# A hand-numbered order, opening only: W, DAD and U products of the first superstep moved ahead of weight pieces and of the second superstep's first key product, a scan and a key load moved later

## The chip, the cores and the metric

One core of one Trainium2 chip runs the kernel. The metric is device time in microseconds (us), median of the runs; lower is better. All times below are us unless marked ns. Engines are called as in the profile: PE is TensorE (matmuls), PEld its weight loads, DVE is VectorE, ACT is ScalarE, POOL is GpSimd, SP is SyncE, which issues every DMA of this kernel.

## The reference

Two parts in a row: a linear-attention recurrence over 768 steps for 4 batches of 8 heads of 40 dimensions, and a feed-forward block on its output.

```
for t in range(S):
    y[:, :, t] = einsum('bhd,bhde->bhe', rt, state)
    Sa = einsum('bhde,bhe->bhd', state, at)
    state_decay = state * wt[:, :, None, :] - einsum('bhd,bhe->bhde', Sa, bt)
    state = state_decay + einsum('bhd,bhe->bhde', vt, kt)
...
x = attn_out.transpose(0, 2, 1, 3).reshape(3072, 320)
h = x @ w_in                      # 320 -> 2048
sp = maximum(h, 0) + log1p(exp(-abs(h)))
return (h * erf(sp)) @ w_out      # 2048 -> 320
```

## The kernel before, in words

**Tiling.** The recurrence is done in chunks of 32 steps. The 32 (batch, head) pairs are two groups of 16; a group's 768 steps are 6 supersteps of 128 steps, so there are 12 supersteps (numbered 0 to 11) of 4 chunks each. The feed-forward block follows one superstep behind: each superstep gives 256 tokens, which go through 16 column tiles of w_in (the products into `ph`, L823), a long ACT and DVE chain, and 16 row tiles of w_out (the products into `po`, L878).

**One superstep.** `prep` loads the decays `w` and makes two scans on DVE (suffix, L439, into `Wt`; prefix, L443 with a copy L444, back into `Pr`). `aphase`, once a chunk, loads the keys (`kba`, tile `bk`), multiplies the a part by the prefix (`ab`, L472) and the k and b part by the suffix (`bk`, L477: "turned keys"), forms the product `A` (L482, into `pA`), masks it (`Am`, L489), sends it to DRAM (`AD`) and transposes the keys (`bT`, L500, also into `pA`, copied out to `sg`). `tphase`, once a superstep, fetches all four chunks' masked products from DRAM (`Ti`), inverts 16x16 triangles by 28 short DVE operations (`Tm` and `Ts`, L529 and L530), sends the result to DRAM (`TD`) and back in another shape (`tb`), turns it by a DVE transpose (`R`, L538), and finishes 32x32 blocks by two groups of PE products with a copy between: `W` (L547, T x Ap into `pA`), `Wm` (the copy into tile `W`, L377), `DAD` (L547 again, Tb x W into `pA`), and `Tb` (a DVE add, L554). `chain`, once a chunk and strictly one after the other, carries the state: `Z` (L593), copy `zt`, `U` (L602: zt x Tb, needs `Tb` of the tphase), copy `us`, `UT` (L627), copy `vtu`, `PQ` (L636), mask `PQm` (L639), `MY` (L647 and L651), and the state add `MT` (L654).

**The opening.** Before the feed-forward block can begin, superstep 0 must go through all of this, and superstep 1's `aphase` and `tphase` run interleaved with superstep 0's four chains. In the same time the weights of the feed-forward block come in as 64 bit numbers and are made into two f32r parts: three integer DVE operations a piece (`w1`, `w3`, `w5`: L737 to L739), a rounding copy on ACT (`whi`, L743, or `whr`, L775), and for each half of a piece the product pair `wd_` on PE (L754 and L755: identity x value, minus identity x rounded value, into `ph` or `po`), copied out by `wlo`. 190 small `warm` products (L422) without a reader are strewn between.

**What sets the order.** Nothing at run time: `Plan.add` only numbers the operations, and `ORDER`, a table of all 4630 numbers, gives the order in which they are issued. Each engine runs its own operations strictly in that order; `ENGINES` says which engine each one runs on.

```
def emission(order):
    with tc.manual_schedule():
        for i in order:
            o = N.P.ops[i]
            o["fn"](o["eng"])
...
for c in range(NC):
    P.add("W", "PE", lambda e, c=c: mm(e, s.AP, W, c, lo), ["T"] + [("ap", j) for j in range(2)], ["pA"], pr, 0.32)
P.add("Wm", [("ACT", 0.37), ("DVE", 0.42)], lambda e: s.copy(e, s.W2[:, :, lo], pw[:, :, lo]), ["pA"], [("w2", 0)], pr)
for c in range(NC):
    P.add("DAD", "PE", lambda e, c=c: mm(e, s.W2, tb, c, up), [("w2", 0)] + ktb, ["pA"], pr, 0.32)
P.add("Tb", "DVE", ...
```

The last number of an `add` is a duration for a planner that is no longer in the file; it has no effect. `A`, `bT`, `W` and `DAD` of all supersteps share the PSUM tile `pA`, so each of them waits until the one before has been copied out.

Of the kernel before, what the change touches and what calls it, by code (L numbers as in the profile page):

```python
# [1008 lines left out]
```

## Time and profile before

| what | value |
|---|---|
| device time, three runs | 767.58, 760.24, 767.63; median 767.58 |
| profiled execution, first to last instruction (span) | 754.8 |
| profiled execution's own time | not given; the page has its span alone |
| PE busy over the span | 722.7 (96%) |
| DVE, ACT busy | 643.1 (85%), 573.3 (76%) |
| DMA | 94.63 MB, mean 125 GB/s |

The page's busy times are of one profiled execution. A busy PE is not a PE at its peak, and among its busy time are the `warm` products, which nobody reads. The span begins with the opening described above, in which PE is mostly filled with such products and everything waits for a chain of small steps; from the first product of the feed-forward block on (L823) PE works without longer pauses until the end.

### The profile page before, as it was taken

To read this page: it belongs to the slowest core of one execution; us is meant where nothing else is said; L and a number is where in the kernel's file an instruction comes from. 1 tells how busy PE (TensorE), PEld (TensorE's weight loads), DVE (VectorE), ACT (ScalarE), POOL (GpSimd) and SP (SyncE) were. 2 spreads that over 40 slices of the span, in tenths; PEclk is the share of its full clock that TensorE was granted. 3 is DMA by queue.
4 is the path that set the end of the run, shared out by engine and by line. 5 is a ranking of instruction groups with operands and counts; after the bars stand their busy time and mean duration, and the time that the engine had idled before them with its cause. 6 is when DMAs were issued, how large, how long until landed. Compare 5 with 4: busy or idle time off the path is not lost.

```text
span 754.8 us, 32087 instructions
## 1 busy us (share of the span) xinstructions
PE 722.7 (96%) x13807; PEld 570.4 (76%) x13807; DVE 643.1 (85%) x1461; ACT 573.3 (76%) x1122; POOL 5.6 (1%) x15
## 2 busy tenths in 40 slices
PE   9968899789999999999999999999999999999996
PEld 3645558668778778878878888887888787888874
DVE  8887878889879899998889899998997898878774
ACT  3322544987988998888898897898988888776992
POOL 2000000000000000000000000000000000000000
PEclk9988999999999999999999999999999999999999
DMA  8687566655564655555545556546545444312000
GB/s 255 175 256 197 142 160 153 144 124 122 129 147 121 131 140 126 118 125 126 131 126 136 132 134 139 130 104 138 140 103 115 124 112 92 104 41 61 21 17 22
DMA packets 165616, 94.63 MB, mean 125 GB/s; under 512 B 115452, under 2 KB 148988, under 8 KB 165468
## 3 DMA queue, kind: packets, MB, share of 16 engines
q1 hardware_dynamic: 165468, 92.51, 50.1%
q8 instruction: 110, 1.80, 1.1%
q14 instruction: 38, 0.31, 0.1%
HBM read 73.48 MB, written 14.16 MB: 116 GB/s over the span
## 4 chain that ended last, share of the span: by engine, by line
PE 83%; ACT 5%; DVE 5%; DMA 3%; issue 2%; SPq 1%; DVEq 0%
PE po L878 29%; PE ph L823 22%; PE my L647 4%; PE ph L422 4%; PE pA L547 4%; PE pQ L636 4%; PE pA L482 3%; PE my L602 2%; PE my L593 2%; PE pA L500 2%; PE pQ L618 2%; PE my L651 2%; SPq L381 1%; PE pQ L627 1%; ACT l L831 1%
## 5 line engine op out<-in xcount | busy, mean ns | idle before, releaser
L878 PE MATMUL po<-wo,h 128*128 128x320 f32 x768 | 265.2, 454 | 1.1 <-DVE h L869 1.1
L878 PEld LDWEIGHTS po<-wo,h 128*128 128x128 f32 x768 | 125.5, 189 | 30.5 <-DVE h L869 1.9
L831 ACT ACTIVATE l<-l 128x512 f32<-128x512 f32 x192 | 111.0, 624 | 8.3 <-DVE nd L856 7.5
L823 PE MATMUL ph<-xh,wih 128*128 128x256 f32 x384 | 113.8, 378 | 0.0
L823 PEld LDWEIGHTS ph<-xh,wih 128*128 128x128 f32 x384 | 69.5, 190 | 24.1 <-issue 0.3
L823 PE MATMUL ph<-xh,wil 128*128 128x256 f32 x384 | 77.2, 282 | 0.7 <-issue 0.7
L823 PE MATMUL ph<-xl,wih 128*128 128x256 f32 x384 | 76.9, 282 | 0.0
L856 DVE TENSOR_TENSOR nd<-l,r 128x512 f32<-128x512 f32 x96 | 64.3, 687 | 9.6 <-ACT r L831 8.4
L868 DVE TENSOR_TENSOR l<-l,r 128x512 f32<-128x512 f32 x96 | 64.5, 682 | 1.2 <-ACT l L831 0.4
L869 DVE SCALAR_TENSOR_TENSOR h<-l,h 128x512 f32<-128x512 f32 x96 | 64.6, 684 | 0.5
L857 DVE SCALAR_TENSOR_TENSOR r<-nd,r 128x512 f32<-128x512 f32 x96 | 64.2, 683 | 0.2
L831 ACT ACTIVATE l<-h 128x512 f32<-128x512 f32 x96 | 57.6, 627 | 4.2 <-DVE h L377 3.1
L823 PEld LDWEIGHTS ph<-xh,wil 128*128 128x128 f32 x384 | 59.5, 190 | 0.7 <-issue 0.7
L375 ACT COPY h<-ph 128x512 f32<-128x512 f32 x84 | 48.9, 583 | 14.2 <-PE ph L823 13.4
L823 PEld LDWEIGHTS ph<-xl,wih 128*128 128x128 f32 x384 | 59.2, 189 | 0.0
L831 ACT ACTIVATE r<-r 128x512 f32<-128x512 f32 x96 | 55.3, 623 | 0.4
L831 ACT ACTIVATE r<-l 128x512 f32<-128x512 f32 x96 | 54.9, 621 | 0.3
L422 PE MATMUL ph<-d 104*128 104x512 bf16 x190 | 53.3, 401 | 1.6 <-DVE d L392 1.6
L823 PE MATMUL ph<-xl,wir 128*128 128x256 f32 x192 | 54.2, 282 | 0.0
L823 PE MATMUL ph<-xh,wir 128*128 128x256 f32 x192 | 54.1, 282 | 0.0
L375 ACT COPY Zm<-MT 40x320 f32<-40x320 f32 x62 | 28.3, 457 | 28.7 <-DVE MT L654 24.1
L489 DVE TENSOR_TENSOR Zs<-pA,tri 64x256 f32<-64x256 f32 x96 | 40.6, 423 | 11.1 <-PE pA L482 6.0
(142 smaller groups left out, 1346.4 us busy)
## 6 DMA issues: line engine op xcount, KB each, us to landing
bk<-in_kba_e SPq DMA_DIRECT2D x46, 416.0 KB
vt<-in_rv_e SPq DMA_DIRECT2D x96, 120.0 KB
wo<-in_moe_w_in SPq DMA_DIRECT2D x10, 512.0 KB
h<-in_moe_w_out SPq DMA_DIRECT2D x10, 512.0 KB
Pr<-in_w_e SPq DMA_DIRECT2D x12, 419.7 KB
Rt<-in_r_e SPq DMA_DIRECT2D x48, 104.0 KB
Vu<-in_v_x SPq DMA_DIRECT2D x96, 40.0 KB
Zm<-in_v_s SPq DMA_DIRECT2D x48, 80.0 KB
```

The costliest lines, as they stand in the source:

```text
L375: self.nc.scalar.copy(o, i)
L422: P.add("warm", "PE", lambda e: nc.tensor.matmul(s.ph[1], s.d1[:, :128], s.d1[:, :512], start=True, stop=True), ["d1"], ["phw"], -1e3, 0.22)
L489: P.add("Am", "DVE", lambda e, x=x, xs=xs: nc.vector.tensor_tensor(out=zx[64:128, x], in0=pz[xs], in1=s.tri[xs, None, :].to_broadcast([64, ...
L547: nc.tensor.matmul(pw[js, i, ts], l[js, i], r[js, i, ts], start=True, stop=True)
L636: nc.tensor.matmul(pq[i % 2 * 64:i % 2 * 64 + 64, i // 4, i // 2 % 2], vr[:, 256 + n_ * 64:320 + n_ * 64], vr.rearrange("p (a x) -> p a x" ...
L823: nc.tensor.matmul(ph[:, j * 256:j * 256 + 256], a[:k, fs], b[:k], start=(m == 0), stop=(m == 7))
L831: self.P.add(name, "ACT", lambda e: nc.scalar.activation(out=o, in_=i, **kw), rd, wr + ["act"], pr, 0.62)
L856: P.add("nd", [("DVE", 0.69)], lambda e, r=r, l=l, nd=nd: s.eng(e).tensor_tensor(out=nd, in0=l, in1=r, op=ALU.mult), [("l", il), ("r", ir) ...
L857: P.add("rho", "DVE", lambda e, r=r, nd=nd: nc.vector.scalar_tensor_tensor(out=r, in0=nd, scalar=2 * C4, in1=r, op0=ALU.add, op1=ALU.mult) ...
L868: P.add("E", [("DVE", 0.69)], lambda e: s.eng(e).tensor_tensor(out=l, in0=l, in1=r, op=ALU.mult), [("r", ir)], [("l", il)], pr)
L869: P.add("G", "DVE", lambda e: nc.vector.scalar_tensor_tensor(out=h, in0=l, scalar=-1.0, in1=h, op0=ALU.add, op1=ALU.mult), [("l", il)], [( ...
L878: nc.tensor.matmul(po, h[:, bs], s.wo[:, f], start=(f == 0), stop=(f == 15))
```

## The change

Only the table `ORDER` changes (and both tables are wrapped at another width, which moves every line number below by 30: L547 of before is L577 after, and so on). 16 numbers of the 4630 stand in another place, all between the 254th and the 386th, that is within the opening. By operation:

- The prefix scan of superstep 1 (463) and its copy come after the 28 short operations of superstep 0's triangle inversion, not before them.
- The load of the second chunk's keys of superstep 1 (476, 416 KB) is issued after the `tb` loads of superstep 0, not before its `TD` stores.
- The four `W` products (310 to 313) stand together, `Wm` (314) follows them on DVE before two weight operations, and the four `DAD` (315 to 318) come next. The two `wd_` pairs of the weight piece with nd (399, 402), which stood before `W` and between `W` and `DAD`, come after `DAD`.
- `U` of chunk 0 (522) with its copy `zt` (521) comes before superstep 1's first `A` (469); it stood after `A`, its mask and `bT`.
- Two warm products, one load of superstep 0's values (537), one store of turned keys (466) and four small weight copies (391, 400, 401, 410) are moved by a few places with them.

```diff
-269 262 463 272 271 362 275 276 372 277 278 279 280 281 282 373 517 283 250 284 285 286 287 288 405 418 289 392 290 291 292 131 293 364 294 295 296 297 273 298 299 462 476 300 301
...
-540 389 135 515 541 421 399 539 516 310 435 425 401 311 312 136 466 313 429 314 402 315 316 317 318 319 410 137 480 138 404 469 400 139 140 471 141 470 391 474 537 477 521 475 522
...
+427 308 380 387 307 476 758 431 134 388 428 465 468 390 309 467 432 540 389 515 541 421 539 516 310 311 312 466 313 135 314 435 425 429 315 316 317
```

On PE around superstep 0's `W` and `DAD`, before (po_164 and po_165 are the halves of the weight piece; L422 is a warm product; the last three are `A`, `bT` and `U`):

```order
L754 MATMUL po_164<-l_133,ident 128x256
L755 MATMUL po_164<-nd_143,nid 128x256
L547 MATMUL pA<-T_106,Ap 32x16 x48
L422 LDWEIGHTS d_114
L422 MATMUL ph_163<-d_114 128x512
L547 MATMUL pA<-T_106,Ap 32x16 x16
L754 MATMUL po_165<-l_133,ident 128x256
L755 MATMUL po_165<-nd_143,nid 128x256
L547 MATMUL pA<-Tb_83,W_104 32x16 x64
...
L482 MATMUL pA<-Ab_76,bk_99 64x2x32 x8
...
L500 MATMUL pA<-ident,bk_99 128x104 x4
L602 MATMUL my<-zt_110,Tb_83 32x40 x16
```

The same place after:

```order
L577 MATMUL pA<-T_106,Ap 32x16 x64
L452 LDWEIGHTS d_114
L452 MATMUL ph_163<-d_114 128x512
L577 MATMUL pA<-Tb_83,W_104 32x16 x64
L784 MATMUL po_164<-l_133,ident 128x256
L785 MATMUL po_164<-nd_143,nid 128x256
...
L784 MATMUL po_165<-l_133,ident 128x256
L785 MATMUL po_165<-nd_143,nid 128x256
...
L632 MATMUL my<-zt_110,Tb_83 32x40 x16
L512 MATMUL pA<-Ab_76,bk_99 64x2x32 x8
...
L530 MATMUL pA<-ident,bk_99 128x104 x4
```

Both weight pairs went from ahead of `DAD` to the stretch between `DAD` and `U`, and `U` from behind `bT` to ahead of `A`; `UT` follows `bT` and two warm products now, as it followed `U` and two warm products before.

On DVE, from superstep 1's prefix scan (Pr_88) over the triangle inversion (Ti) to the copy `Wm` (W_104<-pA), before:

```order
L443 SCALAR_TENSOR_TENSOR Pr_88<-Pr_88,d_115 104x516 x2
L444 COPY Pr_88<-Wt_86 104x8
L529 TENSOR_TENSOR tmp_107<-Ti 128x14
...
L530 TENSOR_TENSOR Ti<-Ti,tmp_107 128x14
L737 TENSOR_SCALAR r_142<-h 128x512
...
L538 STREAM_TRANSPOSE T_106<-Tb_83 128x512
L738 SCALAR_TENSOR_TENSOR r_140<-h,r_140 128x512
L739 SCALAR_TENSOR_TENSOR wo<-h,r_141 128x512
L737 TENSOR_SCALAR r_141<-h 128x512
L739 SCALAR_TENSOR_TENSOR wo<-h,r_142 128x512
L739 SCALAR_TENSOR_TENSOR wo<-h,r_139 128x512
L377 COPY W_104<-pA 128x16x16
```

After:

```order
L559 TENSOR_TENSOR tmp_107<-Ti 128x14
...
L560 TENSOR_TENSOR Ti<-Ti,tmp_107 128x14
L473 SCALAR_TENSOR_TENSOR Pr_88<-Pr_88,d_115 104x516 x2
L474 COPY Pr_88<-Wt_86 104x8
L767 TENSOR_SCALAR r_142<-h 128x512
...
L568 STREAM_TRANSPOSE T_106<-Tb_83 128x512
L768 SCALAR_TENSOR_TENSOR r_140<-h,r_140 128x512
L769 SCALAR_TENSOR_TENSOR wo<-h,r_141 128x512
L407 COPY W_104<-pA 128x16x16
```

The scan went from ahead of the inversion to the stretch between the inversion and `R`; `Wm` passed three weight operations.

## Rows read from the trace of the kernel before

**Rows 1.** The page: the chain's shares by engine, and the key loads.

```profile
PE 83%; ACT 5%; DVE 5%; DMA 3%; issue 2%; SPq 1%; DVEq 0%
...
bk<-in_kba_e SPq DMA_DIRECT2D x46, 416.0 KB
```

**Rows 2.** Chain that ended last, in order of time: start, us, what.

```profile
87.39 3.09 DMA Ti<-AD
...
93.89 0.43 PE po L754 x2
94.33 0.43 PE po L755 x2
...
102.46 4.06 DMA Tb<-TD
...
116.07 1.91 PE ph L823 x16
```

**Rows 3.** Timeline of DVE, ACT and SP, 41 to 61: start, us, engine, line, [idle before].

```profile
41.17 2.35 DVE L443 TENSOR_TENSOR_SCAN Pr<-Pr,d 104x516 f32<-104x516 f32 x2
...
43.62 0.55 ACT L523 ACTIVATE Ti<-cst 128x272 f32<-128x272 f32 x2 [1.30 <-DMA Ti<-AD]
43.63 0.17 DVE L529 TENSOR_TENSOR tmp<-Ti 128x14 f32<-128x14 f32 x1
...
50.30 0.42 DVE L737 TENSOR_SCALAR r<-h 128x512 int32<-128x512 int32 x1
...
51.56 0.43 DVE L737 TENSOR_SCALAR r<-wo 128x512 int32<-128x512 int32 x1 [0.50 <-DMA wo<-in_moe_w_in]
...
55.78 2.38 SPq L381 DMA_DIRECT2D Tb<-TD x2
...
57.03 0.43 DVE L737 TENSOR_SCALAR r<-h 128x512 int32<-128x512 int32 x1 [0.73 <-DMA h<-in_moe_w_out]
...
59.25 0.68 DVE L477 TENSOR_TENSOR bk<-bk,Wt 104x512 f32<-104x512 f32 x1
...
60.95 0.71 DVE L538 STREAM_TRANSPOSE T<-Tb 128x512 f32<-128x512 f32 x1 [1.02 <-DMA Tb<-TD]
```

**Rows 4.** Timeline of PE (and DVE's copy of W), 61 to 72.

```profile
61.98 1.14 PE L547 MATMUL pA<-T,Ap 32*32 32x16 f32 x96
...
63.37 0.44 PE L547 MATMUL pA<-T,Ap 32*32 32x16 f32 x32
...
64.42 0.42 DVE L377 COPY W<-pA 128x256 f32<-128x256 f32 x1
...
64.89 0.59 PE L547 MATMUL pA<-Tb,W 32*32 32x16 f32 x49
...
66.07 0.84 PE L547 MATMUL pA<-Tb,W 32*32 32x16 f32 x79 [0.58 <-issue]
...
66.85 0.60 PE L422 MATMUL ph<-d 104*128 104x512 bf16 x2
...
67.45 0.69 PE L482 MATMUL pA<-Ab,bk 104*64 104x64 f32 x16
...
69.36 0.57 PE L500 MATMUL pA<-ident,bk 104*128 104x104 f32 x4 [0.47 <-DVE Zs L489]
69.86 0.42 PE L602 MATMUL my<-zt,Tb 32*32 32x40 f32 x24
...
70.62 0.27 PE L602 MATMUL my<-zt,Tb 32*32 32x40 f32 x8 [0.34 <-issue]
...
71.36 0.43 PE L627 MATMUL pQ<-ident,Us 128*104 128x128 f32 x2
```

**Rows 5.** Stretches: start:end, us, busy PE, PEld, DVE, ACT, POOL, PE clock, DMA share, GB/s.

```profile
46.00:48.00 2.00, 0.00 (x0) 0.00 (x0) 1.80 (x9) 0.00 (x0) 0.00 (x0) 1.00 0.99 389
...
58.00:60.00 2.00, 2.00 (x5) 1.46 (x6) 1.93 (x4) 0.00 (x0) 0.00 (x0) 0.50 0.67 101
...
62.00:63.00 1.00, 1.00 (x97) 0.99 (x96) 0.96 (x3) 0.89 (x2) 0.00 (x0) 1.00 0.84 222
```

More of the change, by code (lines that the diff above doesn't have):

```diff
@@ L144 @@
-SSSAAPAPVVAAAPAPAPVPVVSSSSSSAAPAPASAAAPAPAPVPVVSSSSSSAAPAPAAAAAPAPAPVPVVSSSSSSSSAAVVVVVVVVVVVVVVVVVVVVVVVVVVVVSSSSVPPPPAPPPPVSVVSAVSSAVPPVAPPAAPPAAPPAAAAAAAAAAAAAAAAVVVVVVVVAAAAAPP
-AAPPAAPPAAVVPPPPPPAAVVPPPPVVPPPPVVPPPPSAVVAVSVSSVPVVSSPVSVSSVPVVSSPASVSSVPVVSSPVSVSSVPVVSSPASSSSSSVAAPAPAVAVVPAPAPVPVVSSSSSSAAPAPAAVVAPVPVPVPVVSSSSSSVVPAPVSSAVPAPAPVPVVSSSSSSAAPAPA
-AAAAPAPAPVPVVSSSSSSSSAAVVVVVVVVVVVVVVVVVVVVVVVVVVVVSSSSVPPPPAPPPPVSAVSAVSSAVAAAAAAAAAAAAAAVVVVVVVVAAAAAPPAAPPAAPPAAVVPPPPPPAAVVPPPPVVPPPPVVPPPPASASAAAAAAAAAAAAAAVVVVVVVVAAAAAPPAAPP
@@ L165 @@
-SSSSVVVPVPVAASAPVPAPVPVVSSSSSSVAPAPASSAVPVPVPVPVVSSSSSSVVPVPVVVVVPVPVPVPVVSSSSSSVAPVPAAASAPVPAPVPVVSSSSVPVVSVVSVVSSVVAAAAAAAAAAAAAAVVVVVVVVAAAAAPPVAPPAAPPVAVVPPPPPPVAVVPPPPVVPPPPVV
+SSVVGVGGGGAAVVGGGGGVVVVGAAAPPPPPPPPPPPPPPPPPPPPPPPPPPPPPPPPPPPPPPPPPPPPPPPPPPPPPPPPPPPPPPPPPPPPPPPPPPPPPPPPPPPPPPPPPPPPPPPPPPPPPPPPPPPPPPPPPPPPPPPPPPP
+PPPPPPPPPPPPPPPPPPPPPPPPPPPPPPPPPPPPPPPPPPPPPPPPPPPPPPPPPPPPPPPPPPPSAVVAVSVSSVPVVSSPASVSSVPVVSSPASVSSVPVVSSPASVSSVPVVSSPASSSSAAVVVVVVVVVVVVVVVVVVVVVVV
+VVVVVSSSSVPPPPVPPPPVSVVVAPAPASVVVAPAPASVVVAPAPVSVVVAPAPASVVVAPAPVSVVVAPVPASVVVAPVPASVVVAPAPASVVVAAAPVAPAASVVVAAAPAVPVVSVVVSVVVSVVVSVVVSVVVSVVVSVVVSVVV
@@ new lines @@
+SVVVSVVVSAVVAVSVSSVPVVSSPVSVSSVPVVSSPASVSSVPVVSSPASVSSVPVVSSPASSSSSSAVPAPAAAVAPAPAPVPVVSSSSSSAAPAPVVAAAPAPAPVPVVSSSSSSAAPAPASAAAPAPAPVPVVSSSSSSAAPAPAA
+AAAPAPAPVPVVSSSSSSSSAAVVVVVVVVVVVVVVVVVVVVVVVVVVVVSSSSVPPPPAPPPPVSVVSAVSSAVPPVAPPAAPPAAPPAAAAAAAAAAAAAAAAVVVVVVVVAAAAAPPAAPPAAPPAAVVPPPPPPAAVVPPPPVVPP
+PPVVPPPPSAVVAVSVSSVPVVSSPVSVSSVPVVSSPASVSSVPVVSSPVSVSSVPVVSSPASSSSSSVAAPAPAVAVVPAPAPVPVVSSSSSSAAPAPAAVVAPVPVPVPVVSSSSSSVVPAPVSSAVPAPAPVPVVSSSSSSAAPAPA
+AAAAPAPAPVPVVSSSSSSSSAAVVVVVVVVVVVVVVVVVVVVVVVVVVVVSSSSVPPPPAPPPPVSAVSAVSSAVAAAAAAAAAAAAAAVVVVVVVVAAAAAPPAAPPAAPPAAVVPPPPPPAAVVPPPPVVPPPPVVPPPPASASAAA
@@ new lines @@
+AAAAAAAAAAAVVVVVVVVAAAAAPPAAPPAAPPAAVVPPPPPPAAVVPPPPVVPPPPVVPPPPSAVVVVSVSSVPVVSSPASVSSVPVVSSPASVSSVPVVSSPASVSSVPVVSSPASSSSSSVVVPAPAAAAAPAPAPVPVVSSSSSS
+AAPAPVAAAVPVPAPVPVVSSSSSSAAPAPAVVSVPAPAPVPVVSSSSSSVAPAPAAASAPAPAPVPVVSSSSSSSSAAVVVVVVVVVVVVVVVVVVVVVVVVVVVVSSSSVPPPPVPPPPVSAVSAVSSVVAAAAAAAAAAAAAAVVVV
+VVVVAAAAAPPAAPPAAPPAAVVPPPPPPAAVVPPPPVVPPPPVVPPPPASVSAAAAAAAAAAAAAAVVVVVVVVAAAAAPPAAPPAAPPAAVVPPPPPPAAVVPPPPVVPPPPVVPPPPSAVVAVSVSSVPVVSSPASVSSVPVVSSPA
+SVSSVPVVSSPASVSSVPVVSSPASSSSSSVAAPAPAAVASPAPVPVPVVSSSSSSVAPAPAASAAPAPAPVPVVSSSSSSAAPAPAAAVSPAPVPVPVVSSSSSSVAPAPASAAAPAPAPVPVVSSSSSSSSAAVVVVVVVVVVVVVVV
@@ new lines @@
+VVVVVVVVVVVVVSSSSVPPPPAPPPPVSVVSVVSSAVAAAAAAAAAAAAAAVVVVVVVVAAAAAPPAAPPAAPPAAVVPPPPPPAAVVPPPPVVPPPPVVPPPPASASAAAAAAAAAAAAAAVVVVVVVVAAAAAPPAAPPAAPPAAVV
+PPPPPPAAVVPPPPVVPPPPVVPPPPSAVVAVSVSSVPVVSSPASVSSVPVVSSPASVSSVPVVSSPASVSSVPVVSSPASSSSSSVVAPAPVVVASPAPAPVPVVSSSSSSAAPAPVAAASPAPAPVPVVSSSSSSAAPAPAAASAPAP
+APVPVVSSSSSSAVPAPVVAVAPVPVPVPVVSSSSSSSSAAVVVVVVVVVVVVVVVVVVVVVVVVVVVVSSSSVPPPPAPPPPVSVVSVVSSVVAAAAAAAAAAAAAAVVVVVVVVAAAAAPPAAPPAAPPAAVVPPPPPPAAVVPPPPV
+VPPPPVVPPPPASASAAAAAAAAAAAAAAVVVVVVVVAAAAAPPAAPPAAPPAAVVPPPPPPAAVVPPPPVVPPPPVVPPPPSAVVVVSVSSVPVVSSPVSVSSVPVVSSPASVSSVPVVSSPASVSSVPVVSSPASSSSSSVAVPAPAV
@@ new lines @@
+VVVPAPVPVPVVSSSSSSAAPAPAAAASPAPAPVPVVSSSSSSAAPAPAAASSPAPAPVPVVSSSSSSAVPVPAAAAAPAPAPVPVVSSSSSSSSAAVVVVVVVVVVVVVVVVVVVVVVVVVVVVSSSSVPPPPAPPPPVSVVSVVSSVV
+AAAAAAAAAAAAAAVVVVVVVVAAAAAPPAAPPAAPPAAVVPPPPPPAAVVPPPPVVPPPPVVPPPPASASAAAAAAAAAAAAAAVVVVVVVVAAAAAPPAAPPAAPPAAVVPPPPPPAAVVPPPPVVPPPPVVPPPPSAVVAVSVSSVP
+VVSSPVSVSSVPVVSSPASVSSVPVVSSPASVSSVPVVSSPASSSSSSVVAPVPAVAVAPVPAPVPVVSSSSSSVVPAPAASASPAPAPVPVVSSSSSSAAPAPASASAPAPAPVPVVSSSSSSVAPAPAAVVSPVPAPVPVVSSSSSSS
+SAAVVVVVVVVVVVVVVVVVVVVVVVVVVVVSSSSVPPPPVPPPPVSVVSVVSSAVAAAAAAAAAAAAAAVVVVVVVVAAAAAPPAAPPAAPPAAVVPPPPPPAAVVPPPPVVPPPPVVPPPPASASAAAAAAAAAAAAAAVVVVVVVVA
@@ new lines @@
+AAAAPPAAPPAAPPAAVVPPPPPPAAVVPPPPVVPPPPVVPPPPSAVVVVSVSSVPVVSSPVSVSSVPVVSSPASVSSVPVVSSPASVSSVPVVSSPASSSSSSVAAPAPVSASVPAPVPVPVVSSSSSSAVPAPAAASVPAPAPVPVVS
+SSSSSAAPAPAASAAPVPAPVPVVSSSSSSAVPAPAAAVVPAPAPVPVVSSSSSSSSAAVVVVVVVVVVVVVVVVVVVVVVVVVVVVSSSSVPPPPAPPPPVSVVSAVSSAVAAAAAAAAAAAAAAVVVVVVVVAAAAAPPAAPPAAPPA
+AVVPPPPPPAAVVPPPPVVPPPPVVPPPPASASAAAAAAAAAAAAAAVVVVVVVVAAAAAPPAAPPAAPPAAVVPPPPPPAAVVPPPPVVPPPPVVPPPPSAVVAVSVSSVPVVSSPASVSSVPVVSSPVSVSSVPVVSSPASVSSVPVV
+SSPASSSSSSVAVPAPAAAAAPAPAPVPVVSSSSSSVVPVPVASASPVPAPVPVVSSSSSSAAPAPAAASAPAPAPVPVVSSSSSSAAPAPASVVVPAPAPVPVVSSSSSSSSAAVVVVVVVVVVVVVVVVVVVVVVVVVVVVSSSSVPP
@@ new lines @@
+PPAPPPPVSVVSVVSSAVAAAAAAAAAAAAAAVVVVVVVVAAAAAPPAAPPAAPPAAVVPPPPPPAAVVPPPPVVPPPPVVPPPPASASAAAAAAAAAAAAAAVVVVVVVVAAAAAPPAAPPAAPPAAVVPPPPPPAAVVPPPPVVPPPP
+VVPPPPSAVVVVSVSSVPVVSSPASVSSVPVVSSPASVSSVPVVSSPASVSSVPVVSSPASSSSSSVVAPAPAAVVAPAPAPVPVVSSSSSSAVPVPASASSPAPAPVPVVSSSSSSAAPAPASASAPAPAPVPVVSSSSSSAAPAPVSS
+AAPAPAPVPVVSSSSSSSSAAVVVVVVVVVVVVVVVVVVVVVVVVVVVVSSSSVPPPPAPPPPVSAVSVVSSAVAAAAAAAAAAAAAAVVVVVVVVAAAAAPPAAPPAAPPAAVVPPPPPPAAVVPPPPVVPPPPVVPPPPVSASAAAAA
+AAAAAAAAAVVVVVVVVAAAAAPPAAPPAAPPAAVVPPPPPPVAVVPPPPVVPPPPVVPPPPSAVVAVSVSSVPVVSSPVSVSSVPVVSSPASVSSVPVVSSPASVSSVPVVSSPASSSSSSVAVPAPVASVVPAPVPVPVVSSSSSSVV
@@ L166 @@
+PAPAAASAPAPVPVPVVSSSSSSAAPVPASSASPVPAPVPVVSSSSSSVVPVPAAVAVPVPAPVPVVSSSSSSSSAAVVVVVVVVVVVVVVVVVVVVVVVVVVVVSSSSVPPPPVPPPPVSVVSVVSSVVAAAAAAAAAAAAAAVVVVVV
+VVAAAAAPPAAPPVAPPAAVVPPPPPPVAVVPPPPVVPPPPVVPPPPVSVSAAAAAAAAAAAAAAVVVVVVVVAAAAAPPVAPPAAPPVAVVPPPPPPAAVVPPPPVVPPPPVVPPPPSSSSSSVVVPVPVAASAPVPAPVPVVSSSSSS
+VAPAPASSAVPVPVPVPVVSSSSSSVVPVPVVVVVPVPVPVPVVSSSSSSVAPVPAAASAPVPAPVPVVSSSSVPVVSVVSVVSSVVAAAAAAAAAAAAAAVVVVVVVVAAAAAPPVAPPAAPPVAVVPPPPPPVAVVPPPPVVPPPPVV
 PPPPVSVSAAAAAAAAAAAAAAVVVVVVVVAAAAAPPVAPPVAPPVAVVPPPPPPAAVVPPPPVVPPPPVVPPPPAAAAAAAAAAAAAAVVVVVVVVAAAAAVVPPPPVVPPPPVVPPPPVVPPPPASAS
```

21 lines of the change are left out of this document (removed), and 268 rows, old and new, of the table ORDER.

## The prediction

> **What bounds the kernel now.** I read the page first, then the chain that ended last, then the timeline of the one stretch that the change touches. PE is busy 96% of the span (the table above) and carries 83% of the chain [rows 1]. So a change that removes no product can win only where PE waits, or where it is filled with warm products while a chain of small steps sets the pace. The chain in order of time shows where that is: up to 116.07, where the first feed-forward product (L823) starts, it runs through scans, short DVE steps, DMA round trips (87.39, 102.46) and small products [rows 2]. From there on PE has its work, and that work is the same before and after. A shift of the opening by d moves the end by about d. The timeline between 41 and 72 then gives the steps that change [rows 3, 4].
>
> The sum is made against the profiled execution, whose span is 754.8. Its own time is not known; the runs shown are 767.58, 760.24 and 767.63. I add the shift to the median, 767.58. The three runs lie 7.4 apart, so about 1% is what a measurement of this kernel can tell from no change. The shifts below are far smaller.
>
> **The scan moved later.** Superstep 1's prefix scan with its copy holds DVE from 41.17 to 43.63, that is 2.46; then the inversion begins [rows 3]. Without the scan it does not begin earlier: its data land just then, as ACT's first step on the same tile shows, which waits 1.30 for that DMA and starts at 43.62 [rows 3]. No gain there. After the inversion, at 50.30, DVE now has the 2.46 first. Between 50.30 and the end of L477 at 59.25 + 0.68 = 59.93 DVE is busy 9.63 less two waits for weight loads, 0.50 and 0.73, so 8.40; then it idles 1.02 until Tb lands and R runs at 60.95 [rows 3]. With the scan the three waits (2.25) are filled: 50.30 + 2.46 + 8.40 = 61.16. R is 0.21 later. Bounds: 0, if the operations close up a little; 1.44 (2.46 - 1.02), if both load waits stay. I take 0.21.
>
> **The key load moved later.** 416 KB leave the queue ahead of TD and Tb [rows 1]; at the 389 GB/s of 46 to 48, when only loads were moving, that is 1.1 [rows 5]. Tb may land about that much earlier, 59.9 for 60.95. It gains nothing, as DVE is not free before 61.16: the wait for the DMA becomes a wait for DVE's own queue. The load itself is now issued behind Tb (at 55.78 and after, 2.38 of issuing), and its first reader is the L477 that follows the add L554, near 67. Tb took from 55.78 to 60.95, 5.2, to be there [rows 3]; a load that goes out near 58 and takes as long lands near 63. Cost 0; if it took twice as long, 1 or so.
>
> **W, Wm, DAD.** R ends near 61.16 + 0.71 = 61.87, so W starts near 61.95, as before (61.98: it stood behind a weight pair that ended then). The 128 products take 1.14 + 0.44 = 1.58 and end near 63.5 [rows 4]. Before, the warm product and DVE's three weight operations put Wm at 64.42; now DVE has only two operations between R and Wm, some 1.4 if they are as long as L477's 0.68 [rows 3], so Wm follows W and starts near 63.55. That is 0.87 earlier, and DAD starts at 64.02 instead of 64.89. This is the gain of the change.
>
> **What then stands between DAD and UT.** The chain of chunk 0 continues when UT (71.36) runs, and UT stands on PE behind all that follows DAD in program order. Before, these were two warm products, A, three warm, the wait for A's mask, bT, U, two warm: 71.36 - 64.89 = 6.47 from DAD's start [rows 4]. After, the same instructions stand there in another order, and in addition two weight pairs and one warm product. A pair takes 0.43 + 0.43 = 0.86 on PE when it runs at the full clock in a dense stretch [rows 2]; the warm product at most 0.30 (0.60 for two) [rows 4]. That is 2.02. Less what now falls out: A no longer waits for the add L554 after the warm products (up to 0.2) and UT no longer for the copy of U's result (0.1). So 6.47 + 1.7 = 8.2, and UT comes at 64.02 + 8.2 = 72.2, 0.85 later than 71.36. U itself is early (near 68.4 instead of 69.86), and that helps nobody, for UT stays behind A, its mask and bT. The keys of superstep 1 fare worse: A starts near 68.8 to 69.6 for 67.45, and its bT near 71.2 for 69.36, but its successors stand behind the chain on PE anyway.
>
> Where would this be cheaper? The second pair ran before between W's end (63.37 + 0.44 = 63.81) and DAD's start (64.89), in which PE had to wait for Wm anyway [rows 4]; the first ran before R was done. Both were covered, and the change takes the cover away. Bounds for this term: 0.3 (the pairs fill a wait for A's mask that I count twice) to 2.0 (nothing falls out).
>
> Within DAD PE pauses 0.58 and within U 0.34 with nothing to wait for [rows 4]. I count both after as before. The Trainium skill (Runtime: NRT & Kernel Launch, Instruction fetch mechanics) says that an engine's instructions are refilled in blocks of 256 and that crossing a block's end is mostly hidden. By that sentence no pause would be there and 0.9 would fall out of before and after alike; these rows disagree on "hidden". The sum goes by the rows.
>
> **The rest.** zt is copied earlier on ACT, the values' load and the turned keys' store go a few places up on SP, four weight copies down: none feeds the first products at 116 late. Cost 0, 0.2 at most.
>
> **Sum.** The terms from DAD's start on, -0.87 + 1.7, give +0.83; R's 0.21 is already within W's start. I take +0.9 at UT. From there to 116 every step of the chain hangs on the one before (MY, MT, the next Z; then Ti at 87.39 and Tb at 102.46 [rows 2]), so it stays 0.9: 767.58 + 0.9 = 768.5, no change that can be measured.
>
> **The rivals.** First, the clock. PE ran at half clock (0.50) from 58 to 60, after it had waited for weight operations, and at 1.00 from 62 on, after it had been busy through 58 to 62 [rows 5]. After, the operations that release the weight pairs come up to 2.46 later, so PE idles longer before R, and the half clock may last into W. Then W's 1.58 doubles and part of the weight pairs too: +1.5 on top, 770.0. Against it: the pairs still run just before W. The Trainium skill (TensorE: Matmul & The Clock Gate, HAM oscillation) says that waits between bursts make the next burst run cold; the 0.50 at 58 agrees.
>
> Second, the delay is taken up before 116, by round trips such as Tb's 4.06 at 102.46, in which the queue and not the issue sets the landing [rows 2]: +0, 767.6. For it: two such trips lie on the chain. Against it: what is queued there moves along with the chain.
>
> Third, faster: Tb lands 1.1 earlier and R follows it, since DVE's stretch from 50.30 shrinks. This decides if DVE needs under 59.9 - 50.30 = 9.6 for scan and weight operations; the rows say 2.46 + 8.40 = 10.86 [rows 3]. It would give R at 59.9, 1.3 ahead of my 61.16: 768.5 - 1.3 = 767.2, not slower.
>
> That the change doesn't do what it says is no rival: the order of instructions shows each move.
>
> **How the numbers follow.** Forecast 0.55, the clock 0.2, taken up 0.15, early R 0.1. None of the four reaches 1% (7.7). That is left to the scatter of the runs: a median that falls to the lower of the levels seen, 760.24, would read as 760.2 + 0.9 = 761.1, or 760 with the third rival. The upper end takes the clock with the upper bounds of the scan's and the pairs' terms: 768.5 + 1.5 + 1.2 = 771. So 760 to 771. The likeliest case alone: 767.7 to 769.7, at the upper level of the runs. Faster by over 1%: 0.07; within 1%: 0.87; slower by over 1%: 0.06.
>
> **What would show it.** Right: DVE reaches R without a wait, near 61.2; Wm within 0.1 of W's end, near 63.6; U near 68.4 and UT near 72.2; the first feed-forward product near 117. Wrong: UT before 71.4 (then the pairs were covered after all); R waiting for Tb; a clock of 0.50 at 62 (the first rival); the first feed-forward product at 116 in spite of a late UT (the second).

## The result: no change that can be measured, and two openings that differ more than the change

The changed kernel takes 766.81 us, median of 19 runs (759.31 to 773.09); the kernel before, in the same rounds, 764.02 (753.5 to 769.24, 19 runs). The ratio is 1.0054, 95% interval 1.0031 to 1.0078. A second set of the changed kernel gave 766.59 against 765.56, ratio 1.0031 (1.0006 to 1.0056). A control, the kernel before against itself, gave 767.54 against 766.90 and yet a ratio of 1.0073 (1.0031 to 1.0115); the ratio leaves out runs that count as disturbed, 7 of 17 on one side there, so by this one control a ratio within about 0.8% of 1 tells nothing here, whatever its interval. The medians put the change at +2.8 and +1.0, and no change at all at +0.6. The forecast was 768.5, between 760 and 771, with a shift of +0.9.

From run to run the time goes with the clock. In the 115 timed runs of the kernel before that have the clock on record, the time falls by 4 to 7 us in each of the four sets for every 0.01 of the mean granted clock; in the control's rounds from 774.80 at 0.966 to 757.14 at 0.995.

The profiled execution of the changed kernel took 759.31 (span 757.4, mean clock 0.984). The page's slices, the kernel after; a slice is 18.9 us, PEclk the granted clock in tenths:

```profile
span 757.4 us, 32089 instructions
...
PE 724.0 (96%) x13807; PEld 572.5 (76%) x13807; DVE 642.6 (85%) x1461; ACT 573.1 (76%) x1122; POOL 5.6 (1%) x15
...
PEclk9986999999999999999999999999999999999999
```

The work is the same as before; only the fourth slice, 57 to 76, has a clock of 0.6. The timeline of DVE, SP and PE through that stretch, the kernel after (the rows that answer to [rows 3] and [rows 4]):

```profile
49.70 2.35 DVE L473 TENSOR_TENSOR_SCAN Pr<-Pr,d 104x516 f32<-104x516 f32 x2
...
49.85 1.15 SPq L411 DMA_DIRECT2D TD<-Ti x2
...
54.00 2.61 SPq L411 DMA_DIRECT2D Tb<-TD x2
...
57.13 1.22 PE L785 MATMUL po<-wih,nid 128*128 128x256 f32 x2 [4.42 <-ACT wih L773]
...
60.30 0.70 DVE L568 STREAM_TRANSPOSE T<-Tb 128x512 f32<-128x512 f32 x1
...
61.06 1.90 PE L577 MATMUL pA<-T,Ap 32*32 32x16 f32 x128 [0.69 <-DVE T L568]
...
63.10 0.42 DVE L407 COPY W<-pA 128x256 f32<-128x256 f32 x1 [0.92 <-PE pA L577]
...
63.58 1.03 PE L577 MATMUL pA<-Tb,W 32*32 32x16 f32 x58
65.75 1.15 PE L577 MATMUL pA<-Tb,W 32*32 32x16 f32 x70 [1.14 <-issue]
66.83 1.22 PE L784 MATMUL po<-l,ident 128*128 128x256 f32 x2
67.84 1.06 PE L785 MATMUL po<-nd,nid 128*128 128x256 f32 x2
...
71.66 0.49 PE L632 MATMUL my<-zt,Tb 32*32 32x40 f32 x32
72.08 0.69 PE L512 MATMUL pA<-Ab,bk 104*64 104x64 f32 x16
...
74.57 0.38 PE L657 MATMUL pQ<-ident,Us 128*104 128x128 f32 x2
...
76.98 0.34 PE L677 MATMUL my<-Vu,sg 64*40 64x72 f32 x8
```

Of the same stretch, the kernel before, TD's store, PE's product behind its longest pause there, and the first MY product:

```profile
50.46 1.16 SPq L381 DMA_DIRECT2D TD<-Ti x2
...
55.86 1.22 PE L755 MATMUL po<-wih,nid 128*128 128x256 f32 x2 [2.54 <-ACT wih L743]
...
73.82 0.34 PE L647 MATMUL my<-Vu,sg 64*40 64x72 f32 x8
```

R (L568) has no wait in front of it; before, it waited 1.02 for Tb. W is one group, `Wm` follows it, DAD follows `Wm`; then come the two weight pairs, U, A, bT and at last UT (L657), at 74.57 for 71.36 before. The stretches of the same trace give the clock (the columns are those of [rows 5]):

```profile
58.00:60.00 2.00, 2.00 (x5) 1.17 (x4) 2.00 (x5) 0.57 (x2) 0.00 (x0) 0.50 0.93 240
60.00:62.00 2.00, 1.31 (x71) 0.94 (x74) 2.00 (x4) 0.00 (x0) 0.00 (x0) 0.50 0.87 209
62.00:64.00 2.00, 1.92 (x106) 1.38 (x102) 1.08 (x4) 0.00 (x0) 0.00 (x0) 0.50 0.83 208
...
68.00:70.00 2.00, 2.00 (x7) 1.37 (x6) 0.42 (x1) 0.60 (x2) 0.00 (x0) 0.50 0.90 285
...
72.00:76.00 4.00, 3.79 (x62) 2.30 (x51) 3.08 (x7) 1.55 (x5) 0.00 (x0) 1.00 0.03 8
```

At 62 to 64 the clock is 0.50, where it was 1.00 before [rows 5]. So W, DAD and both weight pairs ran at 1.2 GHz, and the stretch from R to the first MY product (L677, 76.98) took 16.68 for 12.87. In the chain that ended last the feed-forward block's first product stands at 120.15 for 116.07 [rows 2]:

```profile
120.15 1.91 PE ph L853 x16
```

Read alone, this pair of profiles says that the change costs 4 us and that the first rival, the clock, did it. The experiments were made to test that. The last of them showed that the kernel before can have the same slow opening, so that one profile of each kernel cannot tell what the change does.

### The profile page after: what moved, and what is told of

It reads as the page before. It is cut to its first block, busy times and chain, and to the rows that moved or that the text cites. A ratio compares the mean times of both kernels' runs of the same rounds, so it can differ in the third digit from the quotient of the medians.

```text
span 757.4 us, 32089 instructions
## 1 busy us (share of the span) xinstructions
PE 724.0 (96%) x13807; PEld 572.5 (76%) x13807; DVE 642.6 (85%) x1461; ACT 573.1 (76%) x1122; POOL 5.6 (1%) x15
## 4 chain that ended last, share of the span: by engine, by line
PE 81%; DVE 5%; ACT 5%; DMA 4%; issue 2%; SPq 1%; DVEq 0%; ACTq 0%
PE po L908 27%; PE ph L853 22%; PE my L677 4%; PE pA L577 4%; PE ph L452 4%; PE pQ L666 4%; PE pA L512 3%; PE my L632 2%; PE my L623 2%; PE pQ L648 2%; PE pA L530 2%; PE my L681 1%; SPq L411 1%; PE pQ L657 1%; ACT r L861 1%
```

## The experiments

Marks used below, all read from the traces: TD is the first store of the inverse, R, W, DAD, U, UT as in the text ahead, MY the first product L647 of chunk 0. Numbers in the diffs are those of the table `ORDER`.

**One part at a time.** Three kernels and a filler, run together.

The weight pairs back at their places, the rest of the change kept:

```diff
 wd_ 390
+wd_ 399
 W 310 to 313
+wd_ 402
 DAD 315 to 318
-wd_ 399, 402
 U 522
```

> The changed order, but with the two weight pairs where they stood before (one ahead of W, one between W and DAD). From R to UT it took 10.41 before (60.95 to 71.36) and 14.27 after (60.30 to 74.57). Theory C (clock: the weight pairs that ran just before W had brought PE back to full clock; behind DAD they do it too late): the clock is 1.00 from W on again, R to UT 9.8 to 10.4, time 0.999 to 1.001 of before. Theory O (order alone: PE's queue between DAD and UT is longer, the clock of the one profile is chance): R to UT about 10.3, time 1.000. Theory S (the later scan makes DVE release the pairs late, PE idles, the clock stays low whatever the pairs' place): 0.50 in W and DAD still, R to UT 12.5 to 14, time 1.003 to 1.005.

765.68 against 763.50, ratio 1.0037 (1.0005 to 1.0070). R to UT took 12.73, in theory S's range, and R to MY 15.15: the clock was at 0.50 until 66.87, although the pair 399 ran ahead of W.

The changed order with more warm products ahead of W (15 more by the trace's count):

```diff
-warm 134 x1
+warm 134 x14
...
 wd_ 390
+warm 135 x3
 W 310 to 313
```

> The changed order with 16 extra warm products on PE, 13 ahead of the weight pair that waits for ACT near 57 and 3 ahead of W, so that PE does not stand idle there. Nothing else moves. Theory C: the clock is 1.00 in W and DAD, the pairs behind DAD take 0.87 each, R to UT 11.0 to 11.4, time 1.001 to 1.002 of before: what is left is the price of the order. Theory O: warm products change nothing, time 1.004 to 1.006 as of the changed kernel. Theory S: as C, since it also runs over the clock.

769.45 against 763.50, ratio 1.0070 (1.0039 to 1.0101). R to UT, 14.53, and the time missed what each theory had. W ran at full clock, but DAD was interrupted for 1.96, the clock fell again to 0.50 at 65.28 and the pairs ran at it:

```profile
62.01 1.26 PE L547 MATMUL pA<-T,Ap 32*32 32x16 f32 x128
63.87 0.55 PE L547 MATMUL pA<-Tb,W 32*32 32x16 f32 x43 [0.61 <-DVE W L377]
66.38 1.36 PE L547 MATMUL pA<-Tb,W 32*32 32x16 f32 x85 [1.96 <-issue]
67.67 1.22 PE L754 MATMUL po<-l,ident 128*128 128x256 f32 x2
```

The pairs alone moved, in the order before:

```diff
 wd_ 390
-wd_ 399
 W 310 to 313
-wd_ 402
 DAD 315 to 318
+wd_ 399, 402
```

> The order of before, and only the two weight pairs (with one copy out of the first) moved behind DAD; scan, key load and U stay as before. Theory C: PE idles from the end of the pair into ph (near 60) to W, the clock falls or stays at 0.50 into DAD, R to UT 12.5 to 14.5, time 1.003 to 1.006. Theory O: 1.7 more between DAD and UT and nothing else, R to UT 11.9 to 12.2, time 1.002. Theory S: as O, clock 1.00, since the scan is in its old place.

764.79 against 763.50, ratio 1.0004 (0.9973 to 1.0035); R to UT 13.44 as theory C had it, R to MY 15.90, clock at 0.50 until 71.44. The time lies below theory C's 1.003 to 1.006.

The scan alone moved, in the order before:

```diff
-scanP 463
 triangle inversion 277 to 304
+scanP 463
```

> The order of before, and only superstep 1's prefix scan moved behind the inversion. Theory C: the first weight pair still runs just before W; released up to 2.4 later and at half clock it may end after R and hold W up by 0 to 1.5, the clock is back at 1.00 in DAD; R to UT 10.4 to 12, time 1.000 to 1.002. Theory O: R 0.2 later, R to UT 10.4, time 1.000. Theory S: 0.50 in W and DAD, R to UT 12.5 to 14, time 1.003 to 1.005.

765.53 against 763.50, ratio 1.0024 (0.9990 to 1.0057); R to UT 10.94 as theory C had it, R to MY 13.40, and R itself without a wait, 10.45 behind TD, as in the changed kernel.

The times of these four follow no theory: the kernel that moves the pairs has the slow opening and the time of the kernel before, the one that fills PE is the slowest. The traces suggested a reason for the last. From 60 us on, PE's pauses of over 0.2 us with nothing to wait for stand, but for three of 0.27 to 0.33, at the same one or two places of each 256 instructions of its queue, counted in the trace. In the kernels whose queue has the unchanged number of products and no filler they add up to 4.9 to 7.3 us a run (nine runs, those further below included); in this filled one, whose 15 products more shift every later one against those places, to 11.4.

**The shift, the filler at an even count, and the changed kernel again.**

```diff
-85 warm products at the head, 512 columns
+15 of them as two of 256 columns, 70 of 512
```

> The kernel before, with the first 15 of the 85 filler products at its head cut into two of half the width each: the same columns, but 15 more instructions on PE ahead of everything else. Nothing else is moved. Theory F (positions of the instruction stream): in all traces so far PE's unexplained pauses of over 0.2 us from 60 us on stand at the 192nd or 193rd of each 256 instructions of its queue, 5.4 to 7.4 us of them in a run of the four kernels with 13807 products, and 11.6 us in e2_fill, which has 15 more; so here too they add up to 10 us or more, at other products, and the time is 3 to 5 us above the kernel before (ratio 1.004 to 1.007) at an unchanged mean clock. Rival N (the pauses of e2_fill were chance): 5 to 8 us of pauses, and the time within 1.5 us of the kernel before.

767.08 against 765.56, ratio 1.0042 (1.0010 to 1.0073). The pauses add up to 7.2, inside the rival's 5 to 8 and not at the 10 or more of theory F. Two of them, 0.5 and 0.9, stand where the filled kernel has one too, at its products 6061 and 8347, here one further, and where none of the twelve traces with 13807 products shows one of that length. The second in this kernel:

```profile
439.42 0.33 PE L482 MATMUL pA<-Ab,bk 104*64 104x64 f32 x3 [0.92 <-issue]
```

and in the filled kernel:

```profile
448.15 0.34 PE L482 MATMUL pA<-Ab,bk 104*64 104x64 f32 x4 [1.12 <-issue]
```

So where a pause stands follows the position in PE's queue. That the shift costs time is not shown: the same 15 products more give 7.2 here, within the nine runs' range, and 11.4 in the filled kernel. Why that one is the slowest stays open.

```diff
-85 warm products at the head
+27 products on f32 zeros (two passes each), 16 warm products at the head
...
-warm 134 x1
+warm 134 x14
...
+warm 135 x3
 W 310 to 313
```

> The order and the 15 filler products of e2_fill ahead of W, but with the number of PE's instructions unchanged: 42 of the 85 filler products at the head are dropped and 27 of the others are done on f32 zeros in two passes each, so that the head takes about as long with 70 instructions. Every later instruction stands again where it does in the changed kernel. Theory C (what the change costs is the half clock through the opening), with F for the excess of e2_fill: pauses of 5 to 8 us as in the changed kernel, half clock of the whole run near that of the kernel before (mean clock about 0.983, as e2_fill had, against 0.978 for the changed kernel), and so the time 0 to 2 us above the kernel before, 2 to 4 below the changed one. Theory O (the order alone costs it): the filler brings nothing, 3 to 5 us above the kernel before.

764.43 against 765.56, ratio 1.0008 (0.9977 to 1.0039). As theory C had it, but for two reasons at once: the head also ended earlier, and TD with it (47.54 for 49.85). W ran at full clock, then the clock was at 0.50 from 60.62 to 67.44, over DAD and most of the pairs; from R to MY 15.79.

The same head and filler in the order before:

> The kernel before with the same filler: 15 products more between 51 and 61 us, the same 42 dropped and 27 in two passes at the head, the order of the kernel before otherwise. Theory C: less half clock between 55 and 62 us in those executions in which the kernel before has it for longer; mean clock 0.984 or more, the time 0 to 2 us below the kernel before. Rival: the filler in front of the weight pairs delays them, and R, W and all behind come later by what it takes (15 products of 0.22 us, 3.3 us, less the some 2.5 us that PE idles there): 0 to 2 us above.

762.85 against 765.56, ratio 0.9976 (0.9943 to 1.0009), the only ratio of the study below 1. The clock stays at 1.00 from 51.8 to 748; the stretches show it through the opening:

```profile
52.00:56.00 4.00, 4.00 (x20) 2.50 (x18) 3.71 (x8) 1.46 (x3) 0.00 (x0) 1.00 1.02 271
56.00:60.00 4.00, 2.97 (x106) 2.09 (x104) 2.58 (x5) 0.98 (x2) 0.00 (x0) 1.00 0.86 196
60.00:64.00 4.00, 3.37 (x170) 2.46 (x167) 2.09 (x6) 0.93 (x3) 0.00 (x0) 1.00 0.71 194
```

The changed kernel once more, unchanged:

> The changed kernel once more, for a second profile of its opening and for a comparison on the same chip and in the same rounds as the three others. If the half clock of its first profile (54.4 to 71.4 us) belongs to the order, the opening is at half clock again over W and DAD until the weight pairs have run, and the time from R to the first MY product is again 16 to 17 us, against 12.9 in the kernel before; if it was the luck of that execution, the clock is back by the start of W, and R to MY takes 13 to 14 us. The time is 2 to 5 us above the kernel before.

766.59 against 765.56, ratio 1.0031 (1.0006 to 1.0056). The opening is the first profile's again: clock 0.50 until 71.69, R to MY 16.70. The first half of what was expected held, and it looked as if the half clock belonged to the order; the time, +1.0 by medians, is below the 2 to 5 expected.

**The head alone, a candidate, and the changed order with a short head.**

```diff
-85 warm products at the head, 512 columns
+85 warm products at the head, 428 columns
```

> The kernel before with the 85 filler products at its head cut from 512 to 428 columns each; as many instructions, the same order, no filler added anywhere. In e6_fill_even and e7_before_fill the head ended some 3.3 us earlier than in the kernel before, DVE's idle time of 2.29 us behind it was gone and TD came 2.1 to 2.3 us earlier, so those two runs hold two edits at once. Theory H (the head's filler holds up the first weight pairs): TD again about 2 us earlier, and the time 1.5 to 2.5 us below the kernel before (ratio 0.997 to 0.998). Rival: what is won at TD is lost in front of R or to the clock, the time within 0.8 us of the kernel before, and the gain of e7_before_fill was its filler behind TD.

762.44 against 762.55, ratio 1.0012 (0.9973 to 1.0050). TD came 2.6 earlier, at 47.88, as theory H had it, and all of it was lost in front of R, as the rival had it: DVE waited longer for its loads and for Tb, and R was at 61.27, later than before:

```profile
51.52 0.43 DVE L737 TENSOR_SCALAR r<-wo 128x512 int32<-128x512 int32 x1 [3.04 <-DMA wo<-in_moe_w_in]
57.32 0.43 DVE L737 TENSOR_SCALAR r<-h 128x512 int32<-128x512 int32 x1 [1.05 <-DMA h<-in_moe_w_out]
61.27 0.71 DVE L538 STREAM_TRANSPOSE T<-Tb 128x512 f32<-128x512 f32 x1 [1.05 <-DMA Tb<-TD]
```

Behind R this kernel, which has the order before, ran at 0.50 until 77.49 and took 16.97 to MY. That was the first sign that the half clock is not the changed order's alone.

```diff
 W 310 to 313
+Wm 314
 w1 435, w5 425, w5 429
-Wm 314
 wd_ 402
```

> e7_before_fill (short head, 15 products more between 51 and 61 us, the order of the kernel before), with the W products in one piece and Wm taken up on DVE ahead of three conversion steps (435, 425, 429); the weight pair stays between W and DAD. From R to DAD 3.94 us in e7_before_fill; W takes 1.26 us in one piece at full clock and the pair 1.13, so DAD about 3.1 us behind R, 0.8 us earlier, if DVE's three steps moved behind Wm do not hold up Tb. The time 1 to 4 us below the kernel before (ratio 0.995 to 0.999).

759.92 against 762.55 by medians, ratio 1.0015 (0.9984 to 1.0046), above the 0.995 to 0.999 expected: no gain that is shown. Its opening is the shortest of all, R to DAD 3.32 and to MY 12.37. The two kernels with this head and filler lie 2.7 and 2.6 under the kernel before by their medians, while their ratios lie on both sides of 1. Whether they beat it stays open.

The changed order with the head of 428 columns:

> The changed kernel with the head of e9_short_head, without the filler ahead of W. Theory C: the head gives its 2 us at TD, the opening is still at half clock over W, DAD and the pairs, R to MY takes 16 to 17 us again against 15.8 in e6_fill_even, and the time is 1 to 2.5 us above the kernel before, above e6_fill_even's ratio of 1.0008. Rival: e6_fill_even owed everything to its shorter head and nothing to the clock, and this run has the same ratio as it or a lower one.

763.88 against 762.55, ratio 1.0025 (0.9991 to 1.0058). R to MY 16.28, as theory C has it, but by another way: the clock was at 1.00 from 58.77 to 62.18, so W ran at full clock, and it fell again in DAD, whose pause was 1.85; the pairs ran at 0.50:

```profile
59.14 1.26 PE L547 MATMUL pA<-T,Ap 32*32 32x16 f32 x128 [0.69 <-DVE T L538]
...
63.53 1.15 PE L547 MATMUL pA<-Tb,W 32*32 32x16 f32 x70 [1.85 <-issue]
```

The times of this and of the evenly filled kernel lie too close to tell.

**The control.**

> The kernel before itself, as a control, and for a second profile of its opening. If the half clock through the opening belongs to the changed order alone, the clock is back by the start of W again and R to MY takes 12.9 to 13.4 us. If the order only makes it likelier (e9_short_head and e1_pairs_back have the weight pair ahead of W too, and took 17.0 and 15.2), this execution has it or not as it falls: 12.9 to 13.4 or 15 to 17. The ratio to the kernel before is 1 by nature, so what it shows beside 1 is what such a ratio is uncertain by.

767.54 against 766.90, ratio 1.0073 as told above. Its opening shows what the pair of first profiles could not. The timeline of SP, DVE and PE, the kernel before, second execution:

```profile
50.38 1.16 SPq L381 DMA_DIRECT2D TD<-Ti x2
...
53.17 0.43 DVE L737 TENSOR_SCALAR r<-wo 128x512 int32<-128x512 int32 x1 [2.19 <-DMA wo<-in_moe_w_in]
...
57.48 1.22 PE L755 MATMUL po<-wih,nid 128*128 128x256 f32 x2 [4.23 <-ACT wih L743]
...
62.63 0.71 DVE L538 STREAM_TRANSPOSE T<-Tb 128x512 f32<-128x512 f32 x1 [1.10 <-DMA Tb<-TD]
...
63.59 1.48 PE L547 MATMUL pA<-T,Ap 32*32 32x16 f32 x96
...
66.09 1.22 PE L754 MATMUL po<-l,ident 128*128 128x256 f32 x2
67.10 1.06 PE L755 MATMUL po<-nd,nid 128*128 128x256 f32 x2
68.09 1.90 PE L547 MATMUL pA<-Tb,W 32*32 32x16 f32 x128
...
75.54 0.38 PE L627 MATMUL pQ<-ident,Us 128*104 128x128 f32 x2
...
77.96 0.34 PE L647 MATMUL my<-Vu,sg 64*40 64x72 f32 x8
```

and its stretches:

```profile
60.00:62.00 2.00, 2.00 (x6) 1.42 (x5) 1.53 (x3) 0.00 (x0) 0.00 (x0) 0.50 0.79 115
62.00:64.00 2.00, 2.00 (x35) 1.17 (x38) 1.37 (x3) 0.31 (x1) 0.00 (x0) 0.50 0.70 215
...
72.00:74.00 2.00, 2.00 (x9) 0.99 (x7) 1.54 (x3) 0.00 (x0) 0.00 (x0) 0.50 0.38 150
...
76.00:77.00 1.00, 1.00 (x18) 0.58 (x18) 0.22 (x1) 0.96 (x3) 0.00 (x0) 1.00 0.68 236
```

The same program as that of [rows 3 to 5], and UT is at 75.54, not 71.36, later than in the changed kernel (74.57). W stands behind its weight pair as ever, and runs at 0.50 all the same; R to MY takes 15.32, for 12.87 in the first execution. The first feed-forward product comes at 121.62, against 120.15 and 121.85 in the two executions of the changed kernel:

```profile
121.62 1.90 PE ph L823 x16
```

All openings in one table (us; "clock back" is when the granted clock last rose to 1.00 before 80):

| order | run | TD to R | R to UT | TD to UT | clock back |
|---|---|---|---|---|---|
| before | first profile | 10.49 | 10.41 | 20.90 | 61.98 |
| before | control | 12.25 | 12.91 | 25.16 | 75.52 |
| before | e5_shift | 11.31 | 10.75 | 22.06 | 72.72 |
| before | e9_short_head | 13.39 | 13.16 | 26.55 | 77.49 |
| changed | first profile | 10.45 | 14.27 | 24.72 | 71.44 |
| changed | e8_after_again | 10.44 | 14.29 | 24.73 | 71.69 |
| changed | e11_after_short_head | 10.45 | 13.87 | 24.31 | 69.01 |
| parts | e1_pairs_back | 10.46 | 12.73 | 23.19 | 66.87 |
| parts | e3_pairs_only | 11.63 | 13.44 | 25.08 | 71.44 |
| parts | e4_scan_only | 10.45 | 10.94 | 21.39 | 61.06 |
| filled, changed | e2_fill | 10.45 | 14.53 | 24.98 | 72.10 |
| filled, changed | e6_fill_even | 10.44 | 13.38 | 23.82 | 67.44 |
| filled, before | e7_before_fill | 9.84 | 10.42 | 20.26 | 51.81 |
| filled, before | e10_best | 9.85 | 9.91 | 19.76 | 51.52 |

In e5_shift the clock was at 1.00 from 62.48 and fell once more, from 69.30 to 72.72. In e11_after_short_head, e2_fill and e6_fill_even it had likewise been at 1.00 for W, and fell again at 62.18, 65.28 and 60.62.

The order before gives TD to UT anything from 20.9 to 26.6, mean 23.7 of four; the changed order 24.3 to 24.7, mean 24.6 of three. The difference of the means is 0.9, the forecast's own figure at UT; with a spread of 5.6 among the four, two of them kernels with another head, that is no proof of it. The two kernels themselves have 20.90 and 25.16 before, 24.72 and 24.73 after.

## Why the prediction was right, and where not

**The level.** The sum was made on 767.58, the median of three runs. Over 19 runs the kernel before has 764.02, so the base was 3.6 high. With the later base the same shift gives 764.9, 1.9 under the measured 766.81, where the forecast is 1.7 over it: that the two are equally near is luck. The shift is the fair test: +0.9 forecast, +2.8 and +1.0 by medians, with +0.6 for no change in the control. "No change that can be measured" held. The sum also took it that the end moves as the opening does. From the first feed-forward product to the end the two executions of the kernel before take 638.8 and 639.0, those of the changed kernel 637.3 and 643.1; the rest of the run can scatter by more than the opening was forecast to move.

**The signs.** DVE ran through to R (60.30), and `Wm` followed W (63.10, W ended at 62.97), as the forecast said. U (71.66), UT (74.57) and the first feed-forward product (120.15) came later than its 68.4, 72.2 and 117, and the clock was 0.50 at 62, its sign for the first rival.

**The scan.** DVE runs through to R with no wait, as forecast: 49.70 to 60.30 is 10.60, forecast 10.86. But "R is 0.21 later" was worked out against one execution's waits (0.50, 0.73 and 1.02), as if they had a fixed size. In the control the same waits are 2.19, 0.71 and 1.10, in e9_short_head 3.04, 1.05 and 1.05. In all seven runs with the scan behind the inversion R stands 10.44 to 10.46 behind TD; in the five with it ahead and no filler, 10.49 to 13.39. So the move makes R steady, and gains from nothing to 2.9. The step failed in sign: even against the execution it was read from, R is 0.04 earlier behind TD.

**The key load.** Cost 0 was right as far as R goes: e4_scan_only, which leaves it early, has R 10.45 behind TD as the changed kernel has. Tb is issued 4.80 behind TD there and 4.15 in the changed kernel, and nothing comes of it, for DVE is not free.

**W, Wm, DAD.** The forecast has `Wm` and DAD 0.87 earlier with R 0.21 later, so 1.08 earlier counted from R. Where both orders run at half clock, R to `Wm` is 2.80 and 2.79 in the changed kernel, 3.66 in the control and 3.71 in e9_short_head, a gain of 0.9. In e11_after_short_head, where W ran at full clock, it is 2.14 against 3.47, a gain of 1.33: the products in one group take 1.26, less than the 1.58 counted. DAD gains more at half clock than `Wm` does, R to DAD 3.28 and 3.27 for 5.46 and 5.51, some 2.2, because the pair that stood between W and DAD takes 2.07 there.

**The pairs between DAD and UT.** This term was mis-sized: +1.7, with 2.0 as the upper bound, and a pair priced at 0.86 from a stretch at full clock [rows 2]. From DAD's start to UT the changed kernel takes 10.99 and 11.01, the control 7.45 and e9_short_head 7.65, so some 3.5 more. Of this 1.4 is DAD itself, which takes 3.32 and 3.23 with its pause, for 1.91 in the other two, where it has none. The other 2.1 lies between DAD's end and UT, where the changed kernel runs both pairs at 0.50, 1.9 to 2.1 each. From R to UT the two terms, -2.2 and +3.5, net to +1.2 at half clock (14.28 against 13.04, means of two), for +0.6 forecast at full clock (0.83 less R's 0.21). With R's gain on the other side, the sum came out near the forecast by terms that were each off, which is luck too.

**The pauses.** DAD's pause did not stay as it was: 0.58 in the first profile before, none in the control and in e9_short_head, 1.14 and 1.05 after, 1.85 in e11_after_short_head. The 0.34 within U is gone in the changed kernel.

**The rivals.** The clock rival, at a chance of 0.2 and +1.5, described the profile of the changed kernel: 0.50 at 62, W and pairs slow. Its price was off: W takes 1.90 at 0.50 and 1.26 at 1.00, not the double. So was the point against it, that the pairs still run just before W: both went behind DAD, and PE idled 0.69 ahead of W. Its reason was that PE idles longer before R. What it missed, and the forecast with it, is that the kernel before can do the same. PE's idle time ahead of a weight pair there, near 56, is 2.54 in the first execution, 4.23 in the control, and 4.42 in the changed kernel. [rows 5] shows one execution in which the clock was back as W began, and of the four traces of that order without filler, two have it at 0.50 to 75 and beyond. So the rival prices what an execution can have with either order. Whether the change makes it likelier is not settled. In all six executions with the pairs behind DAD they ran at 0.50, but for the end of the last in two of them; in five of the eight with the pairs ahead of DAD the clock was at 1.00 through W and DAD. That points to the order, but these kernels differ in more than that. And over whole runs, in the second set, the mean clock of the changed kernel is 0.980 (12 runs) and that of the kernel before 0.979 (34 runs). The second rival, that the delay is taken up before 116, is not borne out by the first pair: UT 3.2 later, the first feed-forward product 4.1. The third, an early R, came true in another way than it said: R is earlier than in the typical execution before because nothing is left to wait for, not because Tb lands in less time than DVE needs.

**What stays open.** Why the clock comes back at 62 in some executions of one program and at 75 in others; whether the changed order can keep the full clock through DAD and the pairs (in three executions without filler it had it once, for W and DAD's first products, which proves little); and how much of +1.0 to +2.8 is real.

## What to carry to other kernels

Take a second profile of the unchanged kernel, and a comparison of it with itself, before a difference of a few microseconds between two profiles is explained: here the control differed from the first profile by more than the change did. A wait for a DMA in one execution has no fixed size, so moving work into it can be worth more than the wait that the profile happens to show; a product's price has to be read at the clock of the place it is moved to. When filler is added ahead of a long program, keep the number of instructions the same, or later pauses fall on other products; what that costs is not shown here.

## What the runs showed of the hardware that was not expected

The granted clock of one program in the same stretch is 1.00 from 61.98 in one execution and 0.50 until 75.52 in another, with PE busy in all of 60 to 76 in the second. Before it rose there, PE had run the pairs, W, DAD, A, bT and U; in the first it had run two pairs and half of a third since it last stood idle for over 2 us (55.86).

PE's pauses follow the instruction count: they stand at one or two places of each 256, 0.2 to 2.2 us each, and only at 6 to 11 of 107 such places from 60 us on, most of them behind runs of small products. The Trainium skill (Runtime: NRT & Kernel Launch, Instruction fetch mechanics) gives blocks of 256 instructions whose crossing is mostly hidden; the traces agree for some hundred of them, and put 5 to 8 us a run on the others (11.4 in e2_fill).

The warm products at the head hold up the first weight pairs. In the kernel before, the 85 products let the first pair start only at 22.80; with 428 columns each it starts at 19.05:

```profile
22.80 0.60 PE L754 MATMUL po<-l,ident 128*128 128x256 f32 x2
```

```profile
1.62 17.59 PE L422 MATMUL ph<-d 104*128 104x428 bf16 x85 [1.62 <-DVE d L392]
19.05 0.60 PE L754 MATMUL po<-l,ident 128*128 128x256 f32 x2
```

TD then came 2.6 earlier, and the time was the same.
